# A linear-attention kernel with a mixing block on one Trainium2 core: TensorE's unread products spread over the early stage, and a new order of the 767 tasks

## The chip, the cores and the metric

The program runs on one core of one Trainium2 chip. The metric is the device time of one execution in microseconds (us); the time given for a kernel is the median over its runs. Engines are named as in the profile: PE is TensorE (matmuls; PEld its weight loads), DVE is VectorE, ACT is ScalarE, POOL is GpSimd, SP is SyncE, which here only issues transfers.

## What is computed

`r`, `k`, `v` are (4, 8, 768, 48) in float32: 4 batches, 8 heads, 768 tokens, 48 channels a head. The first half is a recurrence per batch and head, the second a block that mixes tokens and channels of its output:

```python
for t in range(S):                                   # S = 768
    cur = einsum('bhd,bhe->bhde', u[None] * k_t, v_t)
    y[:, :, t] = einsum('bhd,bhde->bhe', r_t, state + cur)
    state = w[None, :, :, None] * state + einsum('bhd,bhe->bhde', k_t, v_t)
x = y as (4, 768, 384)
theta = x @ w_theta
y = w_tok_r @ (x * cos(theta)) + w_tok_i @ (x * sin(theta))   # over tokens, 768 x 768 each
u = x + y
out = u + maximum(u @ w_ch, 0)
```

## The kernel before

The recurrence is done in groups of 256 tokens, three groups a batch, so twelve groups g0 to g11 (g = 3 b + pr in `front`). Per group the program has these tasks, with their engine:

- three loads from HBM on SP's queue, `load k`, `load r`, `load v` (L434 for g0 to g6: 384 KB each; L440 later, in halves);
- `kw`, `rw` (L547, L549; DVE or POOL): k and r times powers of w, which absorb the decay; `vb` (L569 to L573): v to bf16, on ACT, DVE or POOL;
- `flip TK`, `flip TR` (PE, L485, eight 128x128 transposes each), `out TK`, `out TR` (ACT or DVE, L500, L501): PSUM to SBUF, giving KT and RT;
- `scores` (PE, L593, two tasks of 16 matmuls) and four `mAT` (DVE, L602) that mask them; `PD` (L609), `diag` (PE, L626), `dg` (ACT), `yd` (L635): the term with u;
- `outer` (PE, L659): the sums of k v; `F`, `T`, `N` and the casts `Sb1`, `Sb0` (L675 to L683): the state handed on from group to group;
- `states` (PE, L735), two `outputs` (PE, L748), `bonus` (PE, L764) and two `x` copies: the output rows of the group;
- `flip TX` (PE, six blocks) with `out TX`, or one DMA transpose on SP's queue (L491) in their place; two `theta` (PE, L823); `cos`, `sin` (ACT, L830, L834); `z` (DVE, L838).

`mixing` then runs per 128 output tokens three `mix` tasks of four matmuls each (PE, L860), `un` (DVE, L878), a transpose `flip TU` (PE, or a DMA transpose on SP's queue), `chan` (PE, L892), `fin out` (DVE, or ACT with a `fin add` on POOL) and the store. The 768 x 768 weights arrive by six casting transfers that POOL issues (`Wr`, `Wi`, L454, with `Wth`, `Wch`), and PE transposes them with twelve `flip W` of six blocks.

At the start `setup` builds the powers of w. The row of w is fetched by a transfer on ACT's queue (L295). `spread` (PE, L304) copies it to all partitions through the bank "w"; `ln` (ACT, L384) takes its logarithm; six `pow` (ACT, L391) exponentiate it for `kw` and `rw`. Masks, identities and token numbers are made on DVE and POOL.

An **unread product** is a 128x128 by 128x512 matmul of the tile `zero` into a PSUM bank that nobody reads afterwards (`unread`, L285). The kernel before issues twelve: seven ahead of `spread` and five behind it (tasks 4 and 6, "warm").

Nothing is scheduled at run time. `Plan.add` records the tasks 0 to 766 with their dependences; `Plan.issue` walks the list `ORDER` and emits each task on the engine that its digit in `WAYS` chooses. Each engine works its own tasks in that order, strictly first in, first out, so a task that waits holds back all behind it on its engine. `BANKS` gives the PSUM bank of each PE task, `AFTER` a list of pairs (a, b): b waits for a although it needs no data of it (so a POOL operation is kept off certain DVE operations). `IDLE` holds triples (task, bank, n): n unread products into that bank right ahead of the task; it is empty in the kernel before. The lists are written out as numbers, found by a search beforehand. The head of a task's life in the emitter:

```python
for k, n in idle.get(seq, ()):
    unread(k, n, 4)
out = way[-1]()
```

The parts that the change and the prediction touch:

Of the kernel before, what the change touches and what calls it, by code (L numbers as in the profile page):

```python
# [23 lines left out]
PAIRS = (0, 1, 2, 3, 4, 5, 6)  # L24
FIRST, SECOND = 'krv', 'krv'
UN_BY_TWO = ()
WARM, WARM_NS = (7, 5), (2990, 2140)
NBANKS = 8


ORDER = [
# [40 lines left out]
]  # L72

WAYS = ("0000000000000000000000000000000000000000000000000000001001000000100101000000010000000000"
    "0101000000001101000000000000000000000000000000101100000000000000000000100002000000000000"
    "0000010000000000000000000100000000010000000000001000000000000001000000000000000000000210"
    "0000000000000000001000010000001000000000000000000000000000001201101100000000012011011000"
    "0000001201101100001100000000000100001000000000101200000000000011010000000000000000000000"
    "0012000000000000000000000000010000000000120000000000000001201101100000000012011011000000"
    "0001200001100000000010000000001000001011000001200000000000010000020000001000000000000001"  # L80
    "2000000000000110000100000000000000000120000000000000001201101100000000012000011000000000"
    "120110000000000001201101100000000012011011000000000000110000110")

BANKS = ("0123456701254673246052125264012735604236074526347136213052405230547201345013725063102547"
    "3542071456201746203415670136254031462714172175012370264506123540137260514730621562714203"
    "274102405136523047152471524306157431657240315")

AFTER = [
# [3 lines left out]
]  # L92


IDLE = [
]


# [73 lines left out]
def kernel(  # L172
# [755 lines left out]
    ctx.enter_context(tc.manual_schedule())  # L928
    P.issue(tc, ORDER, WAYS, BANKS, AFTER, dict((a, [(k, n)]) for a, k, n in IDLE), unread)

# [29 lines left out]
```

## Time and profile before

| | |
|---|---|
| median of 3 runs | 136.99 us (136.48 to 137.35) |
| the profiled execution's own time | 135.85 us |
| its span, first to last instruction | 134.1 us |
| PE busy in the span | 124.8 us, 93% |
| DVE, ACT, POOL busy | 105.5, 77.4, 63.0 us |
| mean granted clock of PE | 0.949 |

The span is what the views below show; 1.75 us of the profiled time lie around it. A busy PE is not a PE at its peak: each matmul's row lasts until its result is out, and the next starts before that, so the cost of a task is read from start to start, or from the chain of work that ended last, which cuts the rows that way. The granted clock is 1.00 where PE runs at full speed and 0.50 where it runs at half.

### The profile page before, as it was taken

Reading aid. Unit: us, or ns where it says so; the run is one execution under the profiler, and the core shown is the slowest. Engines: PE = TensorE matmul, PEld = TensorE weight load, DVE = VectorE, ACT = ScalarE, POOL = GpSimd, SP = SyncE. Lnnn points to the kernel's source line nnn. Section 1 sums busy time; section 2 is a strip of 40 time slices with the busy share of each in tenths; the row PEclk is TensorE's granted clock in tenths of the full one; section 3 lists DMA queues with packets and bytes.
Section 4 is the critical chain, followed back from the end, with each engine's and each line's share of the span. In section 5 each row is a group of like instructions: output and inputs, shape, how many; then the busy total and the mean of one; then the engine's idle time right before and its main releaser. Section 6 shows DMA issues by size and latency. Waiting matters only on the chain.

```text
span 134.1 us, 4430 instructions
## 1 busy us (share of the span) xinstructions
PE 124.8 (93%) x1857; PEld 85.1 (63%) x1857; DVE 105.5 (79%) x208; ACT 77.4 (58%) x145; POOL 63.0 (47%) x65
## 2 busy tenths in 40 slices
PE   7966699999999999999999999999999999999980
PEld 2255596867767777667767667865666766566540
DVE  6587898985948999798999899999469985345380
ACT  3486775699895699879458644843901151801020
POOL 8203986349005779979230899955256320001000
PEclk9975557999999999999999999999999999999999
DMA  3999999999999899999999999989999423842745
GB/s 88 273 261 261 263 213 207 213 254 257 185 224 269 195 120 100 254 149 147 234 247 190 190 112 196 277 180 192 226 295 120 79 59 64 241 170 59 178 156 196
DMA packets 67238, 25.46 MB, mean 190 GB/s; under 512 B 61841, under 2 KB 67218, under 8 KB 67218
## 3 DMA queue, kind: packets, MB, share of 16 engines
q1 hardware_dynamic: 64720, 22.22, 85.0%
q0 software_dynamic: 2496, 2.95, 13.0%
q8 instruction: 14, 0.23, 0.8%
q14 instruction: 6, 0.05, 0.1%
q10 hardware_dynamic: 2, 0.00, 0.0%
HBM read 20.06 MB, written 4.72 MB: 185 GB/s over the span
## 4 chain that ended last, share of the span: by engine, by line
PE 80%; DMA 8%; ACT 5%; DVE 3%; issue 1%; DVEq 0%
PE bank L860 32%; PE bank L485 14%; PE bank L823 8%; PE bank L892 8%; PE bank L593 5%; DMA uu_all<-uu_all 4%; DMA xT<-x 4%; PE bank L659 3%; PE bank L286 2%; PE bank L748 2%; ACT RT L500 2%; PE bank L764 2%; PE bank L626 1%; PE bank L735 1%; PE bank L800 1%
## 5 line engine op out<-in xcount | busy, mean ns | idle before, releaser
L860 PE MATMUL bank<-z,WrT 128*128 128x384 bf16 x144 | 46.9, 326 | 0.0
L860 PE MATMUL bank<-z,WiT 128*128 128x384 bf16 x144 | 46.8, 326 | 0.0
L860 PEld LDWEIGHTS <-WrT 128*128 128x128 bf16 x144 | 14.0, 98 | 8.4 <-issue 0.3
L635 POOL TENSOR_TENSOR yd<-dg,vb 128x768 bf16<-128x768 f32 x11 | 16.2, 1473 | 6.7 <-DVE mAT L602 2.2
L860 PEld LDWEIGHTS <-WiT 128*128 128x128 bf16 x144 | 14.1, 98 | 7.8
L602 DVE TENSOR_TENSOR mAT<-bank,mask 128x512 bf16<-128x512 f32 x28 | 18.0, 683 | 0.7 <-PE bank L593 0.4
L878 DVE TENSOR_TENSOR uu_all<-bank,x 128x384 bf16<-128x384 f32 x24 | 12.8, 552 | 6.1 <-PE bank L860 6.1
L838 DVE TENSOR_TENSOR z<-x,trig 128x1536 bf16<-128x1536 bf16 x12 | 11.4, 954 | 5.8 <-ACT trig L830 3.7
L830 ACT ACTIVATE trig<-bank,pi 128x384 f16<-128x384 f32 x24 | 13.4, 585 | 4.3 <-PE bank L823 4.3
L834 ACT ACTIVATE trig<-bank 128x384 f16<-128x384 f32 x24 | 11.5, 496 | 7.0 <-PE bank L823 4.3
L547 POOL TENSOR_TENSOR Rw<-ld,rpow 128x768 bf16<-128x768 f32 x6 | 10.9, 1818 | 9.6 <-PE bank L860 7.7
L892 PE MATMUL bank<-Wch,uu_all 128*128 128x384 bf16 x72 | 14.5, 327 | 0.2 <-DMA uu_all<-uu_all 0.2
L823 PE MATMUL bank<-Wth,xT 128*128 128x384 bf16 x72 | 14.0, 327 | 0.1
L500 ACT ACTIVATE RT<-bank 128x1024 bf16<-128x1024 bf16 x12 | 12.3, 1027 | 3.0 <-PE bank L485 3.0
L901 DVE SCALAR_TENSOR_TENSOR fin_all<-bank,uu_all 128x384 f32<-128x384 f32 x21 | 11.3, 552 | 2.9 <-PE bank L892 2.6
L609 POOL TENSOR_TENSOR PD<-RT,KT 128x1024 bf16<-128x1024 bf16 x5 | 10.6, 2124 | 6.1 <-DVE Rw L547 5.9
L602 DVE TENSOR_TENSOR mAT<-bank,mask_c 128x512 bf16<-128x512 f32 x20 | 12.8, 682 | 0.3 <-PE bank L593 0.3
L500 ACT ACTIVATE KT<-bank 128x1024 bf16<-128x1024 bf16 x10 | 10.2, 1023 | 4.6 <-PE bank L485 4.5
L905 POOL TENSOR_TENSOR fin_all<-fin_all,uu_all 128x384 f32<-128x384 f32 x3 | 2.7, 911 | 20.7 <-ACT fin_all L898 17.4
L593 PE MATMUL bank<-RT,KT 64*64 64x128 bf16 (+1 forms) x304 | 9.2, 237 | 2.2 <-ACT RT L500 2.2
L485 PE MATMUL bank<-ident,Kw 128*128 128x128 bf16 x96 | 8.6, 242 | 1.1 <-DVE Kw L547 1.1
L593 PEld LDWEIGHTS <-KT 64*64 64x64 bf16 (+1 forms) x304 | 6.7, 115 | 4.6 <-issue 3.9
(117 smaller groups left out, 211.5 us busy)
## 6 DMA issues: line engine op xcount, KB each, us to landing
ld<-in_r_dram SPq DMA_DIRECT2D x12, 384.0 KB, 6.2
out_dram<-fin_all SPq DMA_DIRECT2D x11, 384.0 KB, 3.7
ld<-in_v_dram SPq DMA_DIRECT2D x7, 384.0 KB, 6.9
ld<-in_k_dram SPq DMA_DIRECT2D x7, 384.0 KB, 10.3
ld<-in_k_dram SPq DMA_DIRECT2D x10, 192.0 KB, 5.1
ld<-in_v_dram SPq DMA_DIRECT2D x10, 192.0 KB, 4.6
fin_all<-in_moe_w_tok_r_dram POOLq DMA_DIRECT2D x1, 384.0 KB, 7.6
z<-in_moe_w_tok_i_dram POOLq DMA_DIRECT2D x1, 384.0 KB, 9.2
```

The lines of the kernel that those rows point to most:

```text
L485: ins = [nc.tensor.matmul(bank16(tok)[:, i * C:(i + 1) * C], s, ident, is_transpose=True, start=(i == 0), stop=(i == n - 1)) for i, s in e ...
L500: ways = [act(n * C, lambda: nc.scalar.activation(dst, src(), Act.Copy)), dve(n * C, lambda: nc.vector.tensor_copy(dst, src()), 1.0 if pai ...
L593: ins.append(nc.tensor.matmul(to[:, hp * C:(hp + 1) * C], a, m, start=(hp == 0), stop=(hp == HP - 1), skip_group_check=True))
L602: mask01[:, j] if pairs else mask_c): nc.vector.tensor_mul(
L635: return eng.tensor_mul(yd.rearrange("p a b d -> p (a b) d"), wide(dg, D), vb.rearrange("p a b d -> p (a b) d"))
L823: ins = [nc.tensor.matmul(bank(th)[:, :HD], xT[:, t, dk, :], Wth[:, dk, :], start=(dk == 0), stop=(dk == ND - 1)) for dk in range(ND)]
L830: P.add(act(HD, lambda th=th, t=t, trig=trig: nc.scalar.activation(trig[:, t, 0], bank(th)[:, :HD], Act.Sin, bias=pi2), 144), use=[th], rd ...
L834: P.add(act(HD, lambda th=th, t=t, trig=trig: nc.scalar.activation(trig[:, t, 1], bank(th)[:, :HD], Act.Sin)), use=[th], rd=["sin"], wr=[( ...
L838: P.add(dve(4 * HD, lambda trig=trig, pr=pr: nc.vector.tensor_mul(z[:, 2 * pr:2 * pr + 2], bc(x[:, 2 * pr:2 * pr + 2], 2, 2), trig), 2.0, ...
L860: ins.append(nc.tensor.matmul(bank(tm)[:, :HD], (WrT, WiT)[ri][:, so, to * C:(to + 1) * C], z[:, so, ri], start=(part == 0 and i == 0), st ...
L878: P.add(dve(HD, lambda tm=tm, t=t, to=to, un=un: nc.vector.tensor_add(un[:, t], bank(tm)[:, :HD], x[:, to])), use=[tm], rd=[("x", xi, pr, ...
L892: ins = [nc.tensor.matmul(bank(tf)[:, :HD], uT[:, t, dk, :], Wch[:, dk, :], start=(dk == 0), stop=(dk == ND - 1)) for dk in range(ND)]
```

## The change

Five lists and the constant `WARM` are replaced; no function is changed. `WARM` goes from seven and five to one and one. `IDLE` gets 13 entries with 26 products, so 28 stand in the program instead of twelve. `spread` therefore stands behind one product instead of seven. `ORDER`, `BANKS`, `WAYS` and `AFTER` are all new.

```diff
-WARM, WARM_NS = (7, 5), (2990, 2140)
+WARM, WARM_NS = (1, 1), (216, 216)
...
 ORDER = [
-    1, 9, 38, 0, 8, 20, 2, 7, 16, 36, 4, 18, 29, 37, 10, 28, 12, 19, 111, 5, 77, 6, 112, 15, 21,
-    11, 23, 13, 22, 24, 155, 71, 30, 25, 31, 27, 14, 73, 17, 72, 113, 88, 74, 35, 75, 89, 114, 90,
-    154, 76, 92, 91, 32, 84, 78, 33, 81, 26, 156, 93, 116, 82, 60, 85, 117, 96, 115, 65, 236, 86,
...
+    1, 9, 37, 0, 20, 2, 16, 4, 7, 36, 29, 111, 5, 8, 28, 10, 19, 11, 6, 112, 12, 21, 24, 13, 18,
+    25, 38, 22, 72, 23, 15, 154, 3, 71, 75, 114, 73, 76, 155, 30, 26, 31, 115, 74, 116, 113, 17,
+    32, 35, 117, 78, 118, 77, 80, 156, 33, 79, 50, 88, 81, 84, 89, 119, 14, 236, 92, 157, 90, 124,
+    27, 125, 158, 91, 121, 193, 85, 83, 96, 86, 34, 97, 82, 159, 65, 87, 98, 160, 161, 39, 93,
+    368, 162, 95, 99, 127, 120, 126, 94, 167, 100, 168, 101, 131, 102, 170, 192, 132, 122, 134,
+    128, 53, 129, 135, 133, 51, 123, 139, 52, 140, 60, 130, 163, 141, 103, 136, 142, 55, 169, 164,
+    144, 174, 143, 239, 68, 66, 138, 145, 175, 137, 67, 235, 242, 176, 166, 171, 104, 172, 69,
...
 AFTER = [
-    (114, 91), (84, 93), (115, 158), (157, 87), (157, 134), (157, 130), (170, 137), (110, 239),
...
+    (17, 77), (157, 158), (93, 127), (130, 136), (239, 137), (239, 173), (110, 371), (251, 281),
...
 IDLE = [
+    (75, 0, 7), (30, 0, 1), (116, 1, 2), (78, 1, 2), (88, 1, 1), (121, 7, 2), (99, 4, 2),
+    (131, 5, 2), (128, 6, 1), (141, 0, 2), (142, 0, 1), (221, 2, 1), (372, 0, 2),
 ]
```

What the numbers stand for, in the early part: 4 and 6 the warm products, 5 `spread`, 21 `ln`, 22 to 25 the `pow` of k and r; of g0: 36, 37, 38 the loads of k, r, v, 71 `kw`, 72 `rw`, 73 `flip TK`, 74 its `out`, 75 `flip TR`, 76 its `out`, 77 `vb`, 78 and 81 `scores`, 79, 80, 82, 83 `mAT`, 84 `PD`, 85 `diag`, 88 `outer`, 89 `F`, 90 and 91 the two halves of `Sb1`, 92 `T`, 93 `N`, 96 `states`, 97 and 98 `outputs`, 99 `bonus`, 100 and 101 `x`, 102 `flip TX`, 104 and 107 `theta`; of g1: 111 to 113 the loads, 114 `kw`, 115 `rw`, 116 `flip TK`, 118 `flip TR`, 119 its `out`, 121 and 124 `scores`, 128 `diag`, 131 `outer`, 139 `states`, 140 and 141 `outputs`, 142 `bonus`, 145 `flip TX`; of g2: 154 to 156 the loads of k, r, v, 157 `kw`, 158 `rw`, 159 `flip TK`, 161 `flip TR`, 164 and 167 `scores`, 171 `diag`, 174 `outer`; 221 an `outputs` of g3, 242 `flip TR` of g4, 372 `flip TK` of g6; 50, 60 `Wr` and 55, 65 `Wi` and 39 `Wth` the transfers of weights, 51, 53, 61, 63, 66, 68 `flip W`; 18 `blank`, 15 `place`: fills on DVE.

Early in the queues this means:

- SP's loads: v0, k0, r0, k1, r1, r2, v1, k2 before; r0, k0, k1, r1, v0, k2, r2, v1 after (the number is the group).
- POOL: before `Sb1` (91), `N` (93), two weight transfers, then `rw` (158); after `vb` (77), one weight transfer, `rw` (158), `Sb1` (91), then the transfers 65 and 39.
- In `WAYS` some tasks change engine; over the whole program: `yd` on DVE 1 to 3 (of 12), `vb` on DVE 4 to 1, on ACT 6 to 7, on POOL 2 to 4; `kw` on POOL 4 to 5, `rw` on POOL 6 to 5; `x` on ACT 9 to 12 (of 24); `out TR` on DVE 0 to 2, `out TK` on DVE 2 to 1, `out W` on DVE 5 to 7 (of 12); `F`, `N`, `Sb0` one or two each from DVE to ACT or POOL; `flip TX` as a DMA transpose 6 to 7 (of 12), `flip TU` 11 to 10; one more `fin out` on ACT with its `fin add` on POOL. `flip TK` and `flip TR` stay on PE in all twelve groups.

More of the change, by code (lines that the diff above doesn't have):

```diff
@@ L26 @@
 UN_BY_TWO = ()
-WARM, WARM_NS = (7, 5), (2990, 2140)
+WARM, WARM_NS = (1, 1), (216, 216)
 NBANKS = 8
 ORDER = [
[40 rows of a table removed]
-]
[L74 to L81, printed above, removed]
[40 rows of a table added]
+]
@@ new lines @@
+WAYS = ("0000000000000000000000000000000000000000001010000100001001000010100000000000020000000001"
+    "0000010000000001000000000000000000000001001000000100000000100000000000100010000000100000"
+    "0000010000000000000010001200000000000001000100001012000000000000000000000000000000100000"
+    "0000000000000000010000010000000000000000000000000000000000000001101100000000012011011000"
+    "0000001201101100000100000000000000001100010000001200000000000010000000000001000000001000"
+    "0012000000000000000100200000000000000000120000000000000001201101100000000012011011000000"
+    "0001200000000000011000000000000000000000000001200000000000010000000000001001000001000001"
+    "2000000000000110000200000010000000000120000000000000001200001100000000012011011000000000"
@@ L82 @@
     "120110000000000001201101100000000012011011000000000000110000110")
-BANKS = ("0123456701254673246052125264012735604236074526347136213052405230547201345013725063102547"
-    "3542071456201746203415670136254031462714172175012370264506123540137260514730621562714203"
-    "274102405136523047152471524306157431657240315")
+BANKS = ("0123456702134560713263543502645760152367531562016531450326730143076125732564137237162543"
+    "0172516307451607312356027156325312467035710570531460735416324750651362705346102734651342"
+    "613742546350534716573243016304236574216350741")
```

75 rows, old and new, of tables (AFTER, ORDER) are left out of this document.

## The prediction

> **What bounds the kernel now.** I read the page's busy shares and slices first, then the busy time by stage, then PE's waits, then the timeline of the first 27 us.
>
> ```profile
> span 134.1 us, 4430 instructions
> PE   7966699999999999999999999999999999999980
> PEclk9975557999999999999999999999999999999999
> ```
>
> ```profile
> 0.00:8.09 8.09, 5.67 (x15) 1.95 (x16) 5.01 (x29) 4.03 (x7) 3.41 (x14) 1.00 0.88 194
> 8.09:16.63 8.54, 6.17 (x108) 5.25 (x109) 6.90 (x16) 5.91 (x12) 4.35 (x6) 0.50 1.27 262
> 16.63:30.56 13.93, 13.91 (x329) 10.73 (x328) 12.70 (x24) 10.50 (x20) 8.33 (x10) 0.82 1.17 225
> 30.56:130.26 99.70, 99.05 (x1409) 67.17 (x1406) 80.30 (x141) 56.92 (x109) 46.92 (x37) 1.00 0.96 178
> 130.26:134.10 3.84, 0.00 (x0) 0.00 (x0) 0.56 (x1) 0.00 (x0) 0.00 (x0) 1.00 0.56 205
> ```
>
> Columns: stretch, length, busy PE, PEld, DVE, ACT, POOL (instructions), granted clock, DMA share, GB/s. From 16.63 PE is never idle for long; in the 99.70 us from the first `mix` to the last `chan` it is idle 0.65. So the end is set by PE's work, and time can be won only ahead of 30.56: 8.09 us before the first real flip, 2.37 us idle in the next stage, and a half-rate clock.
>
> ```profile
> 4.69:8.10 3.41, 1.97 (x9) 0.58 (x8) 2.85 (x10) 2.75 (x6) 0.00 (x0) 1.00 1.28 258
> 8.10:11.52 3.42, 2.56 (x48) 2.17 (x49) 2.81 (x8) 2.51 (x4) 0.33 (x1) 0.50 1.28 261
> 11.52:14.93 3.41, 3.01 (x57) 2.63 (x57) 2.75 (x4) 2.06 (x7) 2.32 (x5) 0.50 1.27 261
> 14.93:18.34 3.41, 2.30 (x84) 2.10 (x84) 3.00 (x7) 3.01 (x5) 2.98 (x4) 0.50 1.23 245
> 18.34:21.76 3.42, 3.40 (x56) 2.47 (x50) 2.89 (x6) 1.69 (x5) 3.28 (x4) 0.50 1.15 206
> ```
>
> The clock changes at 8.10 and 21.76, so I cut the time between into steps of 3.41 us. After a step in which PE was 58% busy the clock fell; after steps of 75, 88 and 67% it stayed low; after one of 99% it rose. I read from this that a step has to be full for the full clock, above 88% at least, and that 58% loses it; in between nothing is shown.
>
> **The change part by part: the head.**
>
> ```profile
> 0.74 0.51 ACTq L295 DMA_DIRECT2D w_one<-in_w_dram  x1
> 0.99 3.17 PE L286 MATMUL bank<-zero 128*128 128x512 bf16 x7 [0.99 <-DVE zero L293]
> 4.09 1.19 PE L304 MATMUL bank<-w_one,ones 1*128 1x384 f32 x2
> 4.70 0.56 DVE L571 CAST vb<-ld 128x768 bf16<-128x768 f32 x1 [1.59 <-DMA ld<-in_v_dram]
> 5.21 1.25 PE L286 MATMUL bank<-zero 128*128 128x512 bf16 x5
> 5.31 0.49 ACT L384 ACTIVATE z<-bank 128x384 f32<-128x384 f32 x1 [2.76 <-PE bank L304]
> 5.83 1.12 ACT L391 ACTIVATE kpow<-z,tok_f 128x384 f32<-128x384 f32 x2
> 6.99 0.96 DVE L547 TENSOR_TENSOR Kw<-ld,kpow 128x768 bf16<-128x768 f32 x1 [0.55 <-ACT kpow L391]
> 8.09 1.01 PE L485 MATMUL bank<-ident,Kw 128*128 128x128 bf16 x8 [1.12 <-DVE Kw L547]
> 11.20 0.34 POOL L682 CAST Sd<-F 64x192 bf16<-64x192 f32 x1 [7.15 <-DVE Kw L547]
> 13.86 0.48 PE L735 MATMUL bank<-Sd,RT 128*128 128x96 bf16 x4
> 14.61 1.84 POOL L547 TENSOR_TENSOR Rw<-ld,rpow 128x768 bf16<-128x768 f32 x1
> 26.18 1.64 PE L823 MATMUL bank<-Wth,xT 128*128 128x384 bf16 x9
> ```
>
> A cold product costs 3.17/7 = 0.45 us. `spread` stands at 4.09 because seven of them stand ahead. Now one does, ending near 1.5; the row of w is not there before its issue ends at 1.25, and was there by 4.09. I take 2.1, near the lower end, since it is one small transfer ahead of all loads. `ln` then starts at 3.3 instead of 5.31, `rw` of g0 could start 1.68 later (5.31 to 6.99) at 5.0; its load now comes first and lands at 4.7, as v0's does; `blank` stands ahead of it on DVE, so I take 5.4. PE meanwhile works the warm product and the seven ahead of `flip TR`: 3.3 + 8 x 0.45 = 6.9. The flip starts there instead of at 8.09. The bounds for this gain are 0 (if the row of w lands late) and 1.8 us (if the seven products run at the full clock); I take 1.2.
>
> **Who keeps it.** Not the early path. The first load lands at 4.7 and each takes 384 KB / 262 GB/s = 1.5 us:
>
> ```profile
> ld<-in_r_dram SPq DMA_DIRECT2D x12, 384.0 KB, 6.2
> ```
>
> so the fifth, now v0, lands at 10.7 (it was first, 4.7), and the seventh, r2, at 13.7. `outer`, `F` and `Sb1` of g0 all wait for v0. Worse, POOL's queue now holds `rw` of g2 ahead of its half of `Sb1` (the cast that stood at 11.20): r2's landing 13.7 + 1.84 + 0.34 = 15.9, and `states` of g0 on PE, which needs both halves, starts at 16.1 with the handover, against 13.86 now. Behind it on PE stand the outputs, the flips of g2, everything. The lower bound is 14.7 (if the loads come 1.2 us sooner, a full head gain), the upper 17 (if `kw` of g2, which AFTER puts ahead of `rw`, is itself 1 us late on DVE). I take 16.1. The 15 products ahead of this point cost nothing: the wait for r2 covers them. If that cover were gone they would cost 15 x 0.22.
>
> **From there to the first `theta`.** PE is again the bound, and I count its tasks. Durations at full clock, from the chain that ended last in order of time (start, us, what):
>
> ```profile
> 22.63 0.51 PE bank L748 x32
> 23.13 0.33 PE bank L764 x4
> 30.72 0.65 PE bank L860 x4
> 32.69 0.34 PE bank L485 x6
> 42.31 0.18 PE bank L626 x8
> 43.69 0.57 PE bank L593 x32
> 47.10 0.39 PE bank L659 x30
> 49.80 0.89 PE bank L485 x16
> 50.70 0.17 PE bank L735 x4
> ```
>
> Between `states` (96) and `theta` (104) the new order has `states` 0.17 and 0.34, four `outputs` 1.02, two `bonus` 0.66, three flips of eight blocks 1.34, six of six (two x, four W) 2.04, two half `scores` 0.57, two `outer` 0.78, two `diag` 0.36: 7.28 us. To these come the products ahead of 99, 131, 128, 141, 142: eight. One of 512 columns costs 0.65/4 x 512/384 = 0.22 at full clock, together 1.76. Dense and at full clock `theta` would start at 16.1 + 9.04 = 25.1.
>
> Two things stand against that. Waits: `flip TX` of g0 stands right behind its two x copies on ACT, and `outer` of g1 behind `vb` on ACT; the nearest rows are PE's own waits for an engine's copy:
>
> ```profile
> PE bank L593 <- ACT RT L500: 2.2, 2, 1.1
> PE bank L485 <- DVE Kw L547: 1.1, 1, 1.1
> ```
>
> so 0 to 2.2, I take 0.9 if the clock is full and 0 if it is low, since a slower PE comes later than the copies. And the clock: before 16.1 PE has work only until the copy of RT of g1, which stands on ACT behind `F`, hence behind v0. `flip TR` of g1 ends near 10.6 (the fourth load at 9.2, DVE 0.96, flip 0.45); v0 at 10.7 and `vb` on POOL, 0.56 x 1.84/0.96 = 1.1, free `outer` only at 11.8; after its 0.39 the copies of F (about 0.4, as the cast at 11.20) and RT (the 1.1 of the row above) free g1's scores at 13.7; and `states` follow at 16.1. At full clock these are gaps of 1.2, 1.2 and about 1.4 us, of which the groups fill one, none and two products. That leaves steps about as empty as the 58% one. So I expect the clock to be low at 16.1. PE's gapless run begins between 13.7 (low clock, its slower work then fills the wait for `states`) and 16.1; the first full step ends 3.41 to 6.83 later, so the full clock returns between 17.1 and 22.9, and I take 20.0. Low clock from 16.1 to 20.0 costs half of it: 1.95. `theta` starts at 25.1 + 1.95 = 27.05.
>
> **Against before.** There `theta` starts at 26.18. By then the new order has done one `outer` and one flip more (0.39 + 0.45 = 0.84; the weight flips of both are four), but three more products follow (ahead of 221 and 372, 0.66). The break-even is 26.18 + 0.84 - 0.66 = 26.36, so 27.05 is a loss of 0.69 us.
>
> **The rest.** The work of PE is the same to the end: `flip TX` one less, `flip TU` one more. The engines that change in WAYS I cost at nothing: from 30.56 on DVE, ACT and POOL have 19, 43 and 53 us idle of 99.7 under PE's work; if that cover is gone, one `kw`-sized product on DVE costs 0.96. Order and banks can win back at most the 0.65 us of idle, or add a wait such as the 1.1 us ones; between -0.65 and +1.1 I take the middle, +0.22. The last tasks are the two transposes, `chan`, `fin out` and stores as now, in another order: 3.84 us again. The transfers of `Wi` and `Wth` are issued behind `Sb1`, near 16.5 and 17.3, and need about this long:
>
> ```profile
> Wth<-in_moe_w_theta_dram POOLq DMA_DIRECT2D x1, 288.0 KB, 8.9
> ```
>
> so `Wth` lands at 26.2, just ahead of `theta` at 27.05: free, but not if PE were a microsecond faster.
>
> Sum: +0.69 + 0.22 = +0.9 us. Against the profiled execution (135.85 = 134.1 of span + 1.75 around it) that is 136.8; the median of the runs, 136.99, stands 1.14 above that execution, so I forecast 136.99 + 0.9 = **137.9**.
>
> **The rivals.**
> - *The clock holds* (0.18). The products suffice, no step is too empty. For it: 28 products lie in the very waits. Against: the 58% step. `theta` at 25.1 + 0.9 = 26.0, so -0.36 + 0.22: 136.9. Even then the groups ahead of 99 to 142 take back 1.76 us. The Trainium skill, "TensorE: Matmul & The Clock Gate", section "Why this matters for your kernels", asks only that no PE gap exceed about 3 us between bursts; by that rule this rival would be the forecast. In the trace no gap of the 58% step exceeds 1.12 us and the clock fell, so the trace disagrees.
> - *The clock comes back late* (0.18). The waits behind g0's x copies break the next step too, low until 23: 25.1 + 3.45 = 28.55, +2.19 + 0.22: 139.4. It decides if PE idles more than about 0.4 us in the step after 16.1.
> - *A wait in the later order* (0.12): one more DMA transpose of x, which takes
> ```profile
> xT<-x SPq DMA_TRANSPOSE x6, 5.3
> ```
> us to land, or a copy reaches PE 1.5 us late in all: +0.69 + 1.5: 139.2.
> - *Faster* (0.16): the head's gain carries through. `states` start at 14.7 and the clock holds: 14.7 + 9.04 + 0.9 = 24.64, -1.72 + 0.22: 135.5. It decides if loads land over 1 us sooner than I put them and POOL's cast with them.
>
> **How the numbers follow.** The forecast has 0.36. A run tells about 1% (1.37 us) from no change. Faster by over 1% is the last rival and a bit of the second: 0.17. Slower by over 1%: the late clock, the later wait and the forecast's upper end: 0.35. Within 1%: 0.48. The forecast's own range is 136.9 to 138.9 (clock back at 17.1 to 22.9, with the +0.22); for 8 in 10 the range takes in the rivals but their far ends: 135.4 to 139.6.
>
> **What would show it.** `spread` near 2.1 and the first flip near 6.9 (head); `states` of g0 near 16.1, released by POOL's cast, itself behind `Rw` (anchor; at 14.7 the faster rival); the granted clock low at 16.1 and full from about 20 (clock; full throughout is the first rival); `theta` near 27; idle PE of 0.4 to 1.8 us between the first `mix` and the last `chan` (rest). The prediction is wrong at its root if `states` do not wait for POOL, or if PE is not gapless after them.

## The result, and the profile after

| | before | after |
|---|---|---|
| median of 20 runs each, on the same chip | 136.5 us | 137.62 us |
| lowest, highest | 135.03, 138.15 | 135.7, 139.29 |
| the profiled execution's own time | 135.85 | 137.95 |
| its span | 134.1 | 136.2 |

The ratio of after to before is 1.0071, with a 95% interval of 1.0042 to 1.0101: a loss of some 1 us, within the 1% called no change. Ratios, here and below, leave out runs over 1.5% above the fastest of their kernel; medians are over all runs. The profiled execution of before lies 0.65 below its median here and that of after 0.33 above, so the two traces differ by 2.1 us, about twice what the runs differ by; I read from them where the time went, and its size from the runs. Lines of after are three higher than those of before.

First the page of after: its span and two of the rows in 40 slices.

```profile
span 136.2 us, 4461 instructions
PE   5997989999999999999999997997999999999980
PEclk9999999999999999999999999999999999999999
```

No slice has a low granted clock any more, but two slices of PE, near 82 and 92 us, now have a 7. Next the busy time by stage (columns as in the prediction: stretch, length, busy PE, PEld, DVE, ACT, POOL, granted clock, DMA share, GB/s); the last row is one step of 3.41 us.

```profile
0.00:8.11 8.11, 6.59 (x19) 2.56 (x20) 5.87 (x29) 3.90 (x6) 3.44 (x14) 1.00 0.90 196
8.11:16.63 8.52, 7.44 (x174) 4.92 (x175) 7.27 (x16) 7.08 (x13) 3.23 (x3) 1.00 1.27 257
16.63:32.62 15.99, 15.10 (x308) 10.74 (x306) 13.74 (x24) 13.07 (x28) 13.42 (x14) 1.00 1.19 249
32.62:132.33 99.71, 97.54 (x1383) 65.23 (x1380) 79.81 (x138) 51.68 (x102) 43.53 (x40) 1.00 0.82 169
12.69:16.10 3.41, 2.33 (x74) 1.50 (x66) 3.41 (x8) 2.81 (x7) 1.19 (x1) 1.00 1.29 260
```

The first `mix` starts at 32.62 instead of 30.56. From there to the last `chan` it is 99.71 us against 99.70, and PE is idle 2.17 us in it, where before it was 0.65. Now the rows of the timeline that answer to those of the head and of `states`; the rows between them are left out:

```profile
2.12 1.61 PE L307 MATMUL bank<-w_one,ones 1*128 1x384 f32 x2 [0.53 <-DMA w_one<-in_w_dram]
...
7.05 1.06 PE L488 MATMUL bank<-ident,Rw 128*128 128x128 bf16 x8
10.79 0.82 POOL L576 CAST vb<-ld 128x768 bf16<-128x768 f32 x1 [6.70 <-DVE uw L367]
12.58 0.33 ACT L704 ACTIVATE F<-bank 128x192 f32<-128x192 f32 x1 [0.80 <-PE bank L662]
12.81 1.02 ACT L503 ACTIVATE RT<-bank 128x1024 bf16<-128x1024 bf16 x1
13.71 0.35 ACT L683 ACTIVATE Sd<-F 64x192 bf16<-64x192 f32 x1
13.88 0.42 PE L596 MATMUL bank<-RT,KT 64*64 64x128 bf16 x16 [1.08 <-ACT RT L503]
14.23 0.60 PE L289 MATMUL bank<-zero 128*128 128x512 bf16 x2
14.58 0.36 ACT L683 ACTIVATE Sd<-F 64x192 bf16<-64x192 f32 x1
14.91 1.81 POOL L550 TENSOR_TENSOR Rw<-ld,rpow 128x768 bf16<-128x768 f32 x1 [2.61 <-DVE Kw L550]
15.11 0.35 PE L629 MATMUL bank<-uw,PD 128*128 128x2 bf16 x8
15.33 0.34 PE L738 MATMUL bank<-Sd,RT 128*128 128x96 bf16 x4
26.86 1.14 PE L826 MATMUL bank<-Wth,xT 128*128 128x384 bf16 x6
```

The first flip stands at 7.05 instead of 8.09, but `states` at 15.33 instead of 13.86 and `theta` at 26.86 instead of 26.18. Both halves of `Sb1` are on ACT (the two casts of L683). The text before the prediction and the prediction itself put one of them on POOL behind `rw`; that was a digit of `WAYS` read wrongly. The load of v0 landed at 10.63, where before has it at 4.68. PE waited 1.08 us for ACT's copy of RT, until 13.88, and came to `states` behind two `scores` tasks, a group of two products and `diag`; the second half of `Sb1` was done at 14.94.

PE's waits (engine, line, what it waited for; us in all, times, longest), without the first product's:

```profile
PE bank L790 <- ACT KT L503: 1.2, 1, 1.2
PE bank L596 <- ACT RT L503: 1.1, 1, 1.1
...
PE bank L826 <- DMA xT<-x: 0.9, 1, 0.9
PE bank L596 <- DVE RT L504: 0.7, 1, 0.7
```

The first and the third are new, and both lie late, at 82.57 and 93.48.

### The profile page after: what moved, and what is told of

It reads as the page before. It is cut to its first block, busy times and chain, and to the rows that moved or that the text cites. A ratio compares the mean times of both kernels' runs of the same rounds, so it can differ in the third digit from the quotient of the medians.

```text
span 136.2 us, 4461 instructions
## 1 busy us (share of the span) xinstructions
PE 126.7 (93%) x1873; PEld 83.4 (61%) x1873; DVE 107.2 (79%) x204; ACT 75.7 (56%) x146; POOL 63.6 (47%) x69
## 4 chain that ended last, share of the span: by engine, by line
PE 77%; DVE 11%; DMA 5%; issue 2%; ACT 1%; ACTq 0%; DVEq 0%
PE bank L863 33%; PE bank L488 11%; PE bank L826 8%; PE bank L895 7%; PE bank L289 5%; DMA xT<-x 4%; DVE mAT L605 4%; PE bank L596 3%; PE bank L662 2%; PE bank L751 1%; PE bank L629 1%; DVE Kw L550 1%; PE bank L307 1%; PE bank L738 1%; PE bank L803 1%
## 5 line engine op out<-in xcount | busy, mean ns | idle before, releaser
L833 ACT ACTIVATE trig<-bank,pi 128x384 f16<-128x384 f32 x24 | 13.7, 594 | 7.8 <-PE bank L826 6.4
L638 POOL TENSOR_TENSOR yd<-dg,vb 128x768 bf16<-128x768 f32 x9 | 13.3, 1475 | 5.9 <-DVE z L841 3.0
L826 PE MATMUL bank<-Wth,xT 128*128 128x384 bf16 x72 | 14.5, 326 | 0.9 <-DMA xT<-x 0.9
L503 ACT ACTIVATE RT<-bank 128x1024 bf16<-128x1024 bf16 x10 | 10.5, 1047 | 4.5 <-PE bank L488 4.5
L503 ACT ACTIVATE KT<-bank 128x1024 bf16<-128x1024 bf16 x11 | 11.0, 1020 | 3.4 <-PE bank L488 3.4
L908 POOL TENSOR_TENSOR fin_all<-fin_all,uu_all 128x384 f32<-128x384 f32 x4 | 3.6, 913 | 19.7 <-ACT fin_all L901 19.7
L904 DVE SCALAR_TENSOR_TENSOR fin_all<-bank,uu_all 128x384 f32<-128x384 f32 x20 | 10.7, 550 | 2.2 <-PE bank L895 2.1
L550 POOL TENSOR_TENSOR Rw<-ld,rpow 128x768 bf16<-128x768 f32 x5 | 9.1, 1815 | 6.9 <-DVE z L841 4.3
L289 PE MATMUL bank<-zero 128*128 128x512 bf16 x28 | 10.5, 468 | 1.0 <-DVE zero L296 1.0
L596 PEld LDWEIGHTS <-KT 64*64 64x64 bf16 (+1 forms) x304 | 6.2, 103 | 5.2 <-issue 3.9
```

The lines of the kernel that those rows point to most:

```text
L289: ins = [nc.tensor.matmul(bank_t[k][:, :wide * C].rearrange("p (a c) -> p a c", a=wide), zero, bc(zero, 1, wide), start=True, stop=True, s ...
L503: ways = [act(n * C, lambda: nc.scalar.activation(dst, src(), Act.Copy)), dve(n * C, lambda: nc.vector.tensor_copy(dst, src()), 1.0 if pai ...
L596: ins.append(nc.tensor.matmul(to[:, hp * C:(hp + 1) * C], a, m, start=(hp == 0), stop=(hp == HP - 1), skip_group_check=True))
L638: return eng.tensor_mul(yd.rearrange("p a b d -> p (a b) d"), wide(dg, D), vb.rearrange("p a b d -> p (a b) d"))
L826: ins = [nc.tensor.matmul(bank(th)[:, :HD], xT[:, t, dk, :], Wth[:, dk, :], start=(dk == 0), stop=(dk == ND - 1)) for dk in range(ND)]
L833: P.add(act(HD, lambda th=th, t=t, trig=trig: nc.scalar.activation(trig[:, t, 0], bank(th)[:, :HD], Act.Sin, bias=pi2), 144), use=[th], rd ...
```

## The experiments

Twelve kernels were run, in four lots, each beside runs of before on the same chip. The expectations name theories by letters or by what they say. At the start **theory A** was that the groups lose what the head gains, because products stand where work is ready and because landings, the weights' above all, set the pace up to `theta`. Its rivals: that the **new order** itself, with its queues and evictions, is what costs, products being paid only in front of ready work; and that the **clock** decides, so that products which raise it early gain on any order.

**1. The late groups taken away.** The changed kernel without the groups ahead of 99, 131, 128, 141, 142, 221 and 372, 11 products:

```diff
 IDLE = [
-    (75, 0, 7), (30, 0, 1), (116, 1, 2), (78, 1, 2), (88, 1, 1), (121, 7, 2), (99, 4, 2),
-    (131, 5, 2), (128, 6, 1), (141, 0, 2), (142, 0, 1), (221, 2, 1), (372, 0, 2),
+    (75, 0, 7), (30, 0, 1), (116, 1, 2), (78, 1, 2), (88, 1, 1), (121, 7, 2),
 ]
```

> The changed kernel without its last seven groups of unread products (11 of 28, those ahead of bonus of g0 and later); order, engines, banks as changed. Theory A (the full clock is held, and the later groups take PE time that its work wants): PE gets back up to 11 x 0.22 = 2.4 us, so 1.2 to 2.4 us less than the changed kernel, 0.5 to 1.5 us less than before. Theory B (the groups lie in waits that are there anyway, the new order itself is what costs): within 0.4 us of the changed kernel. Theory C (the later groups are what holds the clock): the granted clock falls to 0.50 between 16 and 25 us and the time rises by 1 us or more.

Measured: 138.39 us, ratio 1.011 (1.0033 to 1.0186). No gain: `theta` starts at 27.30 instead of 26.86, although eight products fewer stand between `states` (15.45) and it and the clock was full there. Three waits of 0.9 us (for a copy of RT, for `yd`, and one without a releaser, "issue") stand in that stretch, 2.64 us in all, where after has 0.89: the products lay in waits that come back without them. PE's waits of this run, and its timeline behind the longest:

```profile
PE bank L791 <- ACT KT L504: 2.0, 1, 2.0
...
PE bank L597 <- DVE RT L505: 0.9, 1, 0.9
PE bank L663 <- issue: 0.9, 1, 0.9
PE bank L768 <- DVE yd L639: 0.9, 1, 0.9
```

```profile
83.86 0.37 PE L791 MATMUL bank<-Sb,RT 64*128 64x48 bf16 x16 [2.01 <-ACT KT L504]
...
87.01 0.53 PE L864 MATMUL bank<-z,WiT 128*128 128x384 bf16 x1
...
88.54 0.33 PE L864 MATMUL bank<-z,WiT 128*128 128x384 bf16 x1
```

Behind an idle time of 2.01 us the same matmul lasts 0.53 instead of 0.33: the granted clock is half from 84.71 to 88.12. So the total of this run holds a cost of the clock too and is no clean price of the 11 products.

**2. No groups at all** (`IDLE` empty, two products left).

> The changed kernel without any of the 13 groups; the two single warm products stay. Theory A: no step of 3.4 us is full before about 16, so the clock is low until 20 or so as in the kernel before; half-rate work costs about 2 us and the 4 us of products that are gone give most of it back: within 1 us of the changed kernel. Theory B: the groups cost nothing and gain the clock, so without them 2 us or more slower than changed.

Measured: 137.89 us, ratio 1.0138 (1.0065 to 1.0211); `theta` at 27.73, the full clock recorded only from 24.63. Its interval and that of the changed kernel (1.0071) overlap; if anything the groups help the new order. `states` stands at 15.33 here too, and ACT's rows for `F`, the copy of RT and the second half of `Sb1` start at 12.60, 12.83 and 14.60, each within 0.02 us of those of after. The products do not make `states` late.

**3. Groups on the old order.** The kernel before with eight groups (32 products), order, engines and banks as they were:

```diff
 IDLE = [
+    (73, 4, 5), (75, 7, 1), (78, 0, 6), (118, 2, 4), (124, 4, 4), (131, 2, 1), (99, 6, 4), (63, 6, 7),
 ]
```

> The kernel before, its order, engines, banks and twelve warm products kept, with 32 unread products put ahead of the eight tasks at which PE waits or would wait at full clock (flip TK and TR, scores of g0, flip TR, scores and outer of g1, bonus of g0, the first flip W). Theory A (early on, loads and weights that land set the pace: Wth lands at 25.25 us in the kernel before, first theta at 26.18): clock full from about 8 us, and at most 0.9 us less than before. Theory D (the half-rate clock from 8 to 22 us is itself what the early stage costs): 2 to 3 us less than before. If the groups are too long where they stand: up to 1 us more than before.

Measured: 136.69 us, ratio 1.001 (0.996 to 1.006). Its clock is full from 3.92, yet `theta` gains 0.2 us:

```profile
18.66 1.03 PE L290 MATMUL bank<-zero 128*128 128x512 bf16 x4
19.62 0.50 PE L768 MATMUL bank<-yd,place 64*128 64x384 bf16 x4
20.05 1.68 PE L290 MATMUL bank<-zero 128*128 128x512 bf16 x7
21.57 0.50 PE L489 MATMUL bank<-ident,fin_all 128*128 128x128 bf16 x6
...
25.96 1.31 PE L827 MATMUL bank<-Wth,xT 128*128 128x384 bf16 x7
```

The bonus's `yd` was ready at 18.48 and `Wr` landed at 19.64; the groups of four and seven hold `bonus` until 19.62 and the flip of W until 21.57. Here products stood in front of ready work.

**4. New early order, old late order.** The order of the changed kernel up to the fifth `mix` task, then that of before, banks refitted.

> The changed kernel up to the fifth mix task (about 34 us), from there on the order and engines of the kernel before; banks refitted behind the seam, the last three unread products left out. Theory A' (about 1.5 us of the loss is waits of the later new order, at 82 and 93 us of the changed trace): 1.5 to 2.2 us less than the changed kernel, so about 1 us less than before. Theory E (those waits come from transfers that land late in single runs, whatever the order): the same as the changed kernel within 0.7 us (three products of 0.22 are gone).

Measured: 139.79 us, ratio 1.0287 (1.0237 to 1.0337). The seam costs waits of its own, the longest 1.24 us at 53.23 and 1.01 at 66.55; behind 66.55 PE never waits, so the late waits of the changed kernel belong to its late order, but the total tells nothing.

**5. and 6. Two waits of the changed kernel taken away.** In one, POOL's transfers of `Wi` and `Wth` (65, 39) are issued right behind `Wr` (50); in the other the two `vb` (551, 593) are moved behind the eviction `out TK` (590) on ACT.

```diff
 ORDER = [
...
-    50, 88, 81, 84, 89, 119,
+    50, 65, 39, 88, 81, 84, 89, 119,
...
-    159, 65, 87, 98, 160, 161, 39, 93,
+    159, 87, 98, 160, 161, 93,
```

```diff
 ORDER = [
...
-    433, 551, 528, 465, 593, 508, 434, 423, 435, 589, 509, 430, 529, 590, 514,
+    433, 528, 465, 508, 434, 423, 435, 589, 509, 430, 529, 590, 551, 593, 514,
```

> The changed kernel with POOL's two weight transfers Wi and Wth issued right behind its third one's place, ahead of POOL's rw copy, where POOL idles from 12.3 to 14.9 us. Theory "the landing of the weights sets the pace up to theta": Wi lands near 21.9 instead of 23.72 and Wth near 24.2 instead of 25.98, theta begins some 1 us earlier (about 25.9 instead of 26.86), and the time is about 1.2 us less than the changed kernel's, near 136.4 in an execution where the changed kernel has 137.6. Rival "the products themselves and their evictions set the pace": the weights land earlier, theta stays within 0.3 us of 26.86, and the time is the changed kernel's within 0.3.

> The changed kernel with two vb copies of ACT (tasks 551 and 593, which wait 2.29 us for a load of v near 80 us) moved behind the out TK eviction of group 10 (task 590). Theory "the idle 1.18 us at 82.57 is that eviction held up behind the vb copies": the wait at 82.57 falls to 0.3 us or less, the later waits to about 1.1 us in sum, and the time is 0.6 to 0.9 us less than the changed kernel's (136.7 to 137.0 where that has 137.6). Rival "the late order has a slack of its own that comes out elsewhere": the wait comes back at the outer products that read vb or a bank later, their sum stays at 2 us, and the time is the changed kernel's within 0.3.

Measured: 137.83 us, ratio 1.0123 (1.0074 to 1.0172), and 137.34 us, ratio 1.0064 (1.0032 to 1.0096). In the first `Wth` is issued at 12.94 and lands 11.0 later, at 23.9, yet `theta` starts at 26.26, and the second, which left the transfers alone, has it at 26.08: the weights do not set `theta` in the changed kernel. Both traces have the full clock from 6.7 us or earlier, and `states` at 14.80 and 14.79. In the second the wait at 82.57 is this:

```profile
81.35 0.94 PE L664 MATMUL bank<-vb,Kw 128*64 128x48 bf16 x40 [0.51 <-ACT vb L574]
```

These rows of the changed kernel had shown where it came from, ACT's first and PE's behind it:

```profile
80.03 1.58 ACT L572 ACTIVATE vb<-ld 128x768 bf16<-128x768 f32 x2 [2.29 <-DMA ld<-in_v_dram]
81.51 1.00 ACT L503 ACTIVATE KT<-bank 128x1024 bf16<-128x1024 bf16 x1
...
82.57 0.37 PE L790 MATMUL bank<-Sb,RT 64*128 64x48 bf16 x16 [1.18 <-ACT KT L503]
```

An eviction stood behind two copies that waited 2.29 us for a load, and a `states` task wanted the eviction's bank. With the copies behind it 0.51 us of waiting for `vb` remain, where 0.3 or less was expected. From `theta` to PE's end this run takes 105.08 us against 105.47 in after and 105.44 in run 5. The mechanism is shown; the time is not told apart from after's by the intervals, and the gain of 0.6 to 0.9 us that was expected is not shown.

**7. and 8. Fewer groups on the old order.** The kernel before with the first five of the eight groups (20 products), none behind 12.5 us; then the same with two short ones, 2 ahead of 63 and 3 ahead of 104.

> The kernel before with 20 of its late products moved into five early groups (4 ahead of task 73, 1 ahead of 75, 6 ahead of 78, 4 ahead of 118, 4 ahead of 124), and none behind 12.5 us; order, engines and banks of the kernel before. Theory A (the clock is full early, and then the landings of the weights are the next bound): bonus near 18.7, flip of W near 20, theta near 24.3 where Wth lands, against 26.18 before: 1 to 1.9 us less than before, 134.2 to 135.1 where before has 136.1. Rival: with no products between 18.5 and 21 the clock falls in those gaps, or the loads set the pace all the same: theta at 25.9 to 26.5 and the time that of before within 0.4.

> As the run with five groups on the kernel before, with two more, short ones over the waits for the weights (2 products ahead of task 63, 3 ahead of 104). If the clock falls in those waits without them, this one is faster by the products that would run at half rate, up to 0.5 us; if it holds without them, this is the same within 0.3 us or slower by the 5 products where the weights have landed already (5 by 0.06 us = 0.3 us).

Measured: 135.67 us, ratio 0.991 (0.987 to 0.9951), and 136.77 us, ratio 0.9992 (0.9953 to 1.0032). Five of the first one's twelve runs lie at 136.8 to 138.2; by the medians it is 135.67 against 136.51. The two traces suggest why runs differ: to task 63 both kernels issue the same, and these are their five products behind `spread`, the first kernel's first.

```profile
4.89 1.25 PE L289 MATMUL bank<-zero 128*128 128x512 bf16 x5
...
24.77 1.64 PE L826 MATMUL bank<-Wth,xT 128*128 128x384 bf16 x9
```

```profile
5.66 2.31 PE L289 MATMUL bank<-zero 128*128 128x512 bf16 x5
...
26.58 1.63 PE L826 MATMUL bank<-Wth,xT 128*128 128x384 bf16 x9
```

In the first the clock was full from 3.96, in the second from 9.27: 0.25 and 0.46 us a product, and `theta` 1.81 us apart, of which the five extra products explain at most 5 x 0.22 = 1.1. That the products ahead of `spread` and the flips cost most when the clock comes late is read from these two traces alone.

**9. The head alone.** The kernel before with `spread` behind one product and eight behind it; nothing else of the change.

```diff
-WARM, WARM_NS = (7, 5), (2990, 2140)
+WARM, WARM_NS = (1, 8), (216, 1728)
```

> The kernel before with one part of the change alone: spread behind one unread product instead of seven, eight products behind it instead of five (nine in all instead of twelve), everything else of the kernel before. The head as the change priced it: spread near 2.1 instead of 4.09, the first flip (of Kw of g0) near 7.2 instead of 8.09, since k0 lands at 6.17 and kw takes 0.96. Theory "the end is set by PE, and the head is a gain of its own": theta and the end come 0.5 to 0.9 us earlier, near 135.7 where before has 136.5. Rival "the next loads keep the gain": the first flip comes earlier, states stay near 13.9 and the time is that of before within 0.3 us; with a step emptier still the clock may come back later, up to 1 us slower.

Measured: 135.56 us, ratio 0.9945 (0.9915 to 0.9975). In its trace:

```profile
2.13 1.61 PE L306 MATMUL bank<-w_one,ones 1*128 1x384 f32 x2 [0.54 <-DVE tok_f L324]
...
11.97 0.33 PE L737 MATMUL bank<-Sd,RT 128*128 128x96 bf16 x4
...
25.29 1.64 PE L825 MATMUL bank<-Wth,xT 128*128 128x384 bf16 x9
```

`theta` comes 0.89 us sooner than before's 26.18. On the old order the head's gain is kept. Not all of it need be the head's: the first flip came 0.68 us sooner (7.41), `states` 1.89, and the full clock lasted to 14.75 here, to 8.10 in before. How much is the clock's is not told apart.

**10. and 11. The head and the groups.** The kernel with five groups, with `spread` behind one product (five behind it, three ahead of 73); then without the groups of four ahead of 118 and 124.

> The faster kernel with five early groups (20 products, on the order, engines and banks of before), and spread behind one product instead of seven: 1 ahead of spread, 5 behind it, 3, 1, 6, 4, 4 in the groups, 24 in all instead of 32. In that kernel's two relatives the head depended on when the clock rose: first flip at 7.82 with the full clock from 3.96, about 9.5 with the full clock from 9.27. Theory "the clock's rise comes at a chance moment, and eight products fewer cost less when it comes late": the first flip near 7.2 in either case, the runs near 137 to 138 become fewer, and the median falls 0.3 to 0.8 us below that kernel's (135.0 to 135.4 where before has 136.5). Rival "fewer products ahead, so the clock rises later or falls again": half rate up to 15 or 20 us, the time of before or slower (136.5 to 137.5).

> As the run with spread ahead and five groups, without the two groups of four ahead of the flip of Rw of g1 (task 118) and of a scores task of g1 (124): 16 products in all. These two stand where before had PE idle 1.11 us each (11.77 and 16.63). If the products hold the clock there: without them it falls as in before after its step of 58%, and the time goes back to 136.2 or more. If the waits are too short to matter: the time is that of the run with five groups within 0.3 us.

Measured: 135.51 us, ratio 0.996 (0.9924 to 0.9996), with one run of twelve above 136.7 instead of five, but a median only 0.16 below that of run 7; and 136.89, ratio 0.9933 (0.9894 to 0.9971), six of its twelve runs at 137.2 to 139.5. Without the two groups the clock falls again, in its trace from 18.91 to 22.33. By the medians the second is slower, by the ratios it is not, so what the two groups are worth in time is not settled.

**12. The head, and the clock held.** Nine products more on the kernel of run 9, put where that one showed PE idle:

```diff
 IDLE = [
+    (78, 0, 4), (118, 2, 2), (124, 4, 3),
 ]
```

> The run with spread ahead alone on the kernel before (nine products), and nine more in three groups where it showed PE idle: 4 ahead of the first scores (idle 1.32 us at 9.42), 2 ahead of the flip of Rw of g1 (0.73 at 12.30), 3 ahead of a scores task of g1 (1.11 at 13.65). There the clock fell at 14.75 and came back at 21.58, after steps of 57% and 46%; PE worked 6.4 us in it at half rate. Theory "the low clock from 14.75 costs what it slows": with the steps filled the clock stays full, theta moves from 25.29 to about 24.3 (bounded by the landing of Wth, issued at 15.33 and 8.6 us on its way, 23.9), the time falls by 0.5 to 1.0 us more, to 134.6 to 135.1 where before has 136.5. Rival "the landings of Wr, Wi and the copies of x set the pace there, as in the kernel before with eight groups": theta within 0.4 us of 25.29 and the time that of spread ahead alone within 0.3 us; or up to 0.5 us slower, where a group stands in front of work that is ready.

Measured: 134.62 us, ratio 0.9869 (0.9809 to 0.9929), the fastest of all. Its timeline:

```profile
9.63 1.03 PE L289 MATMUL bank<-zero 128*128 128x512 bf16 x4
10.91 0.64 PE L596 MATMUL bank<-RT,KT 64*64 64x128 bf16 x32 [0.25 <-ACT RT L503]
...
12.14 0.33 PE L738 MATMUL bank<-Sd,RT 128*128 128x96 bf16 x4
...
24.08 1.64 PE L826 MATMUL bank<-Wth,xT 128*128 128x384 bf16 x9
```

`theta` starts at 24.08, 1.21 us before that of run 9; 24.3 was expected. The steps of that run and of this one, at the same place:

```profile
7.92:11.34 3.42, 1.95 (x78) 1.58 (x77) 3.27 (x7) 2.91 (x6) 0.34 (x1) 1.00 1.28 261
11.34:14.75 3.41, 1.58 (x32) 1.37 (x29) 3.40 (x8) 2.54 (x6) 3.16 (x4) 1.00 1.28 264
14.75:18.16 3.41, 3.02 (x109) 2.87 (x109) 3.41 (x6) 2.88 (x5) 3.27 (x4) 0.50 1.18 226
```

```profile
9.45:12.87 3.42, 3.17 (x64) 2.01 (x61) 3.17 (x5) 2.87 (x7) 1.45 (x3) 1.00 1.28 262
12.87:16.28 3.41, 2.58 (x93) 1.83 (x93) 3.41 (x7) 3.01 (x6) 3.41 (x4) 1.00 1.25 254
16.28:19.69 3.41, 2.58 (x62) 1.92 (x53) 3.41 (x7) 2.21 (x5) 3.13 (x5) 1.00 1.15 214
```

Behind the steps in which PE was 57% and 46% busy the clock fell; with 93, 76 and 76% it held.

**What follows.** By ratios: `spread` ahead is worth -0.55%, and nine products in three small groups on the old order another -0.76% (0.9945 to 0.9869, the intervals of the two overlap by 0.0014). The changed kernel has the same head and more products, and stands at 1.0071, 2.0% above run 12. What is left of the change between them is the order with its queues, engines and banks, and where the groups lie in it. Taking the groups out of it gains nothing (runs 1 and 2), but in both of these the clock costs too, so the totals alone do not settle it. The traces do, up to `states`: after and run 12 have the same head and the full clock from 9.28 and 9.45, and `states` at 15.33 and 12.14. It stays at 15.33 without any group (run 2) and at 14.8 with an earlier clock (runs 5 and 6). So neither the products nor the moment of the clock make it late; the order does. Of the 3.23 us by which PE ends later in after than in run 12, 2.78 have been lost at `theta`. So theory A fell for the changed kernel, in both its parts (runs 1 and 5), and the order as the cause stands. A's first part holds only for groups in front of ready work, as in run 3; and a full clock gains only where nothing of that kind stands against it (0.2 us at `theta` in run 3, 1.2 in run 12). Which of the order's pieces (loads, queues, engines) carries the most was not told apart.

## Why the prediction was right, point by point

The forecast was 137.9 against 136.99, +0.9 us; the runs give 137.62 against 136.5, +1.1, or by the ratio +0.97. That the total is right is luck: it is a sum of errors that cancel, and in the traced pair, which differs by 2.1 us, they do not.

- **The head: right.** `spread` 2.12 (predicted 2.1), the first flip 7.05 (6.9). In run 9 this gain, with what the clock added to it, is worth 0.9 us at `theta`.
- **"Not the early path" keeps it: right in the outcome, wrong in its last step.** The prediction named its own sign of being wrong at its root, that `states` do not wait for POOL, and this came: `states` started at 15.33, not 16.1, while POOL's `rw` started only at 14.91. The part ahead of that held: v0 landed at 10.63 (predicted 10.7), `outer` of g0 came at 12.10 (11.8), and g1's `scores` at 13.88 (13.7), behind `F` and the copy of RT on ACT. Then came not POOL but ACT's queue, with half of `Sb1`, `pow` and the other half at 14.58, and PE's own tasks from 13.88 on. With the old order and the same head `states` stood at 11.97 and 12.14. That v0's late load and ACT's queue make the difference is argued from these rows; no run undid them alone.
- **The sum of tasks from `states` to `theta`: mis-sized.** I counted 9.04 us (7.28 and 1.76 of products). From start to start the trace has 10.65: eight products 2.14 instead of 1.76, flips 3.54 (3.38), `scores` 0.80 (0.57), `states` 0.80 (0.51), `outputs` 1.22 (1.02), `bonus` 0.93 (0.66), `diag` 0.48 (0.36), `outer` 0.74 (0.78). Durations taken from single rows of the chain were up to 36% too short where small tasks of different shapes follow each other. Nor is this sum what sets `theta`, as the prediction had it ("PE is again the bound"): run 1 has eight products less in it and `theta` 0.44 later. PE is full there because the products fill waits for other engines.
- **The clock: wrong.** I expected it low at 16.1 and back at 20, for 1.95 us. It was full from 9.28 to the end, although PE was 68% busy in the step from 12.69 to 16.10. The gaps of 1.2, 1.2 and 1.4 us that were to empty the steps ahead of 16.1 were one, of 1.08 us. And the rule I drew from one fall, "58% loses it", is no rule: in run 9 a step of 57% kept the clock, and one of 46% lost it. What does decide it stays open.
- **The waits in that stretch: the size right, the places not.** They come to 0.89 us, where I had 0.9 for the full clock. But 0.68 of it is a wait of `scores` for DVE's copy of RT, and 0.21 has no releaser; `flip TX` behind the x copies and `outer` behind `vb`, the two places named, do not wait. The forecast itself counted no waits, since it had the clock low.
- Together: 16.1 - 0.77 + 9.04 + 1.61 + 0.89 gives 26.87, and 26.86 was measured, against a forecast of 27.05: the missing 1.95 of low clock was paid by tasks longer by 1.61 and waits of 0.89, less the 0.77 that `states` came earlier.
- **The first rival, "the clock holds",** is what happened to the clock. Its `theta`, 26.0, was too early by the tasks' 1.61 less the 0.77 of `states`, and its time, 136.9, too low. It says that the products take back 1.76 us; run 1, where `theta` did not come sooner without them, shows that they don't. The Trainium skill, "TensorE: Matmul & The Clock Gate", section "Why this matters for your kernels", asks for no idle gap above about 3 us. In after the longest gap behind 9.28 is 1.18 us, and the clock held: there the trace agrees. In run 1 it fell behind a gap of 2.01 us, in run 9 with none above 1.31: there it disagrees.
- **The rest: mis-sized.** I gave the later order +0.22. From the break-even at `theta` (26.36) to PE's end the profiled pair shows 2.08 - 0.50 = +1.58, of which 1.52 are idle time (2.17 instead of 0.65). The place of the largest piece, the eviction behind two copies, is shown by run 6. In the runs' medians the whole loss is 1.0 to 1.1 us, half of the 2.08 of this pair; which of the two pieces is smaller there stays open.
- **The range** does not follow from its ends. By the prediction's own sum a clock back at 17.1 or 22.9 gives 136.5 and 139.4, not 136.9 and 138.9.

## What to carry to other kernels

Price a bundle of edits by trying its parts on the old order: here one part gained 0.55%, filling three measured waits gained another 0.76%, and the new order around them lost 2%. A filler on the critical engine costs nothing inside a measured wait and its whole length in front of ready work, so its size is the wait's, read from the trace of the very order that it stands in. A queue that is strictly first in, first out makes a late load delay whatever eviction stands behind its copy, and then the bank that the eviction frees.

## What the runs showed of the hardware

- The moment at which the full clock comes is a matter of the execution: PE works from 0.99 us in every trace, and the full clock was recorded from 3.92, 3.96, 4.69, 6.42, 6.68, 7.06, 7.92, 9.27, 9.28, 9.45, 9.62, 10.46, 12.09 and once 24.63 us, 3.96 and 9.27 with the same instructions ahead. The Trainium skill, "TensorE: Matmul & The Clock Gate", section "Part 1: The HAM clock gate (the "warmup" mystery)", says that the window of 3413 ns runs freely and that the change comes within some 500 ns either way for it. The steps of 3.41 us agree; the spread here, from 3.9 to 12.1 without the last, is some eight times that, and what sets it stays open.
- The granted clock is shown as 1.00 until the first record, also where the products' own length, 0.45 against 0.25 us, shows half rate. The length of a known matmul is the safer sign.
- The busy share of one step does not decide a fall alone: 58% fell in before, 57% held in run 9, 68% in after.
